# A fused attention and two-layer MoE kernel: the planner's transfer costs, the due times of v and the release of weight loads

## The chip, the cores and the metric

The kernel runs on one core of a Trainium2 chip. The metric is the device time of one execution in microseconds (us). The core's engines run side by side and meet through semaphores: TensorE (PE, with its weight loads as PEld), VectorE (DVE), ScalarE (ACT), GpSimd (POOL) and SyncE (SP), which here only issues transfers. Each engine takes its own instructions strictly in order.

## The reference

Channel attention over 6016 tokens and 256 channels, and two feed-forward layers on its output. All arrays are float32; the weights of the layers arrive as 8-byte numbers that the kernel converts itself.

```python
qn = q / (norm(q, axis=1) + 1e-6)          # 6016 x 256
kn = k / (norm(k, axis=1) + 1e-6)
a = softmax(kn.T @ qn / tau)               # 256 x 256
x = v @ a                                  # 6016 x 256
h = x @ w_in1;  g = relu(h) ** 2           # 256 -> 2048
x = g @ w_out1                             # 2048 -> 256
h = x @ w_in2;  g = maximum(0.01 * h, h)
out = g @ w_out2
```

## The kernel before

The attention matrix is folded into the first layer's w_in, so that the first layer starts from v. From there on the tokens go through in six groups p of two halves, most of 512 tokens a half (`WIDTH`). For each layer L and group p there is a sweep over eight units g, each of 256 of the 2048 inner channels. A unit multiplies x by its part of w_in in seven products (`F1` to `F7`, a Strassen-like form; each product is three matmuls, since every number is split into a high and a low part), applies the nonlinearity on VectorE and ScalarE, and multiplies by its part of w_out into four banks y that a whole sweep adds up. A unit is 45 matmuls. Only the first sweep (layer 1, group 0) has a plain form with four products and a hand-written order.

Beside the units, each sweep of layer 1 has to make the x of the next group (`prepare_x`): two halves of v are loaded, each in four transfers (`load_v`, L236), transposed on VectorE (L245), combined (L1154, L1157) and split into high and low (L1148 on ScalarE, L116 on VectorE) in the single tile xr. It also takes the y of the group before out of its banks into a tile o (`take_out`) and stores it (`put`); v and o share a pool of three buffers. In the second sweep, each wi tile is loaded back (L1185), its sums are made (`join`, L1190) and it is stored again. The second layer's weights are loaded (`load`, L144), converted on VectorE and ScalarE (`exponent` to `low`, tags wst, ce, cm, whl, wis) and stored, which has to be done before the second layer begins.

All this is ordered ahead of time by a planner in the kernel's Python. Every step is a `Task` with an engine, a cost, a due time and what it depends on; a `Buf` is one use of a buffer from a pool, and `link` makes each use wait for the users of the buffer so many places before it, in order of due times, and not start before the use just before it. `simulate` then plays all engines: an engine takes, of the tasks that are ready, the one that is due first. The unit of time is one matmul. A task's followers on other engines are ready at its end and its `lat` later. The plan's start times give the order in which the instructions are emitted, and so the order on each engine; the planned times themselves are not on the chip.

```python
x = min((x for x in open_[e] if x.ready <= t), key=lambda x: x.due)
...
d.ready = max(d.ready, x.end + (0 if d.engine == e and x.lat < 1 else x.lat))
```

Transfers are tasks on SP. Before the change each has the cost 1 and the flight time `LOAD` = 22, but for the load of x in layer 2, which has 2.5 times 22.

Of the kernel before, what the change touches and what calls it, by code (L numbers as in the profile page):

```python
# [31 lines left out]
def attn_moe_moe2(  # L32
# [16 lines left out]
    T = N // P  # L49
# [249 lines left out]
    ACT, DVE = "ACT", "DVE"  # L299
# [31 lines left out]
    with (  # L331
# [46 lines left out]
        for n, (t0, g) in enumerate(tiles):  # L378
            t = qk.pop(n)
# [69 lines left out]
        y, m, z, r = (small[:, i] for i in range(4))  # L449
# [298 lines left out]


    tasks, lines = [], {}  # L750

    class Buf:

# [5 lines left out]
    class Task:  # L759


        def __init__(self, engine, cost, due, fn, *args, deps=(), alloc=None, uses=(), lat=0.3):
            self.engine, self.cost, self.due, self.fn, self.args = engine, cost, due, fn, args
            self.deps = [x for x in deps if x is not None]
            self.order, self.lat, self.start = [], lat, None
            self.item = None
            if alloc is not None:
                alloc.alloc = self
                alloc.users.append(self)
            for b in uses:  # L770
                b.users.append(self)
            tasks.append(self)
# [12 lines left out]
    def simulate(pe):  # L785
        for x in tasks:
            x.then, x.then_order = [], []
        for x in tasks:
            x.left, x.ready = len(x.deps) + len(x.order), 0
            for d in x.deps:  # L790
                d.then.append(x)
            for d in x.order:
                d.then_order.append(x)
        free = {"DVE": 13, "ACT": 6, "SP": 0, "PE": 0}
        open_ = {e: [] for e in free}
        for x in tasks:
            if not x.left:
                open_[x.engine].append(x)
        n = len(tasks)
        while n:  # L800
            best = None
            for e in ("DVE", "ACT", "SP"):
                if open_[e]:
                    t = max(free[e], min(x.ready for x in open_[e]))
                    if best is None or t < best[0]:
                        best = t, e
            t = pe.when(free["PE"])
            if t is not None and (best is None or t < best[0]):
# [12 lines left out]
            for d in x.then + x.then_order:  # L821
                d.left -= 1
                if x in d.order:
                    d.ready = max(d.ready, t)
                if x in d.deps:
                    d.ready = max(d.ready, x.end + (0 if d.engine == e and x.lat < 1 else x.lat))
                if not d.left and d.engine != "PE":
                    open_[d.engine].append(d)
        return free

    KEEP = 4
    LOAD = 22
    GAPS = {"F2": 1, "F3": 1, "F4": 2}

    class PE:
# [72 lines left out]
    def build(base):  # L908
# [10 lines left out]
        def T(*a, **k):  # L919
            return Task(*a, **k)  # L920
# [18 lines left out]
        def convert(u, due, loaded=None, first=None, pace=4, begin=0):  # L939
# [2 lines left out]
            blocks = u.blocks  # L942
            if loaded is None:
                w = Buf("wst", 3, d(-12))
                t = T("SP", 1, d(-12), u.load, alloc=w, lat=LOAD, deps=[begin] if begin else ())
                deps = [t]
            else:
                w, deps = loaded, ()
# [28 lines left out]
                t = T("ACT", 2.7, d(5), u.round, deps=[t], alloc=to, uses=[cm])  # L977
                t = T("DVE", 3, d(6), u.low, deps=[t], uses=[cm, to])
            if u.kind == "o" or L == 2:
                stores[u.kind, L, g] = T("SP", 1, d(7), u.store, deps=[t], uses=[to], lat=LOAD)  # L980
            return t

        whl_done = {0: None, 1: None}
# [15 lines left out]
        for n in range(NG):  # L999
# [3 lines left out]
            if g + 1 < NG:  # L1003
                pw = {}
                b = wi_b[1, 0, g + 1] = Buf("wi", 3, at0(m["fold"]))
                t = T("PE", 6.4, at0(m["fold"]), lambda g=g, pw=pw: pw.update(enumerate(fold(g + 1))),
                      deps=[whl_done[g + 1], *pw_after], alloc=b, uses=[whl_b[g + 1], eT_b])
                fixed.append(t)
                hi = [T("ACT", 2.1, at0(m["fold_high"] + 2.2 * i), lambda i=i, pw=pw: fold_high(i, *pw[i]), deps=[t], uses=[b])
                      for i in range(KC)]  # L1010
                lo = [T("DVE", 2.5, at0(m["fold_low"] + 2.6 * i), lambda i=i, pw=pw: fold_low(i, *pw[i]), deps=[hi[i]], uses=[b])
                      for i in range(KC)]
                pw_after = lo
                stores["i", 1, g + 1] = T("SP", 1, at0(m["fold_low"] + 6), store_folded, g + 1, deps=lo, uses=[b], lat=LOAD)
# [50 lines left out]
        def finish_plain(L, p):  # L1065
# [4 lines left out]
            for half in range(2):  # L1070
# [8 lines left out]
                else:  # L1079
                    a = T("ACT", 2.7 * s, due, take_out, key, 0, deps=done[L, p, half, 0], alloc=o)  # L1080
                b = T("DVE", 3.1 * s, due + 0.1, take_out, key, 1, deps=done[L, p, half, 1] + [a], uses=[o])
                stores["y", L, p, half] = T("SP", 1, due + 3, put, key, deps=[a, b], uses=[o], lat=LOAD)
                if (L, p) == (1, NP - 1) or p < NP - 1:
                    q = (L, p + 1) if p < NP - 1 else (2, 0)
                    for d, t in enumerate((a, b)):
# [7 lines left out]
        def prepare_x(L, p):  # L1093
# [17 lines left out]
            if L == 1:  # L1111
                vs = []
                for half in range(2):
                    v_b[p, half] = Buf("v", 3, t0 + (46, 76)[half])
                    vs.append(T("SP", 1, t0 + (46, 76)[half], load_v, p, half, alloc=v_b[p, half], lat=LOAD))
                for j, (kc, half) in enumerate(((0, 0), (1, 0), (0, 1), (1, 1))):
                    i = SLOT[kc, half]

# [9 lines left out]
            else:  # L1128
# [1 line left out]
                    new()  # L1130
                    nc.sync.dma_start(raw_x(0, 4), x2_d[p][:, :, :w])

                t = T("SP", 1, t0 + 30, load, alloc=xr, lat=2.5 * LOAD, deps=[stores["y", 1, p, 0], stores["y", 1, p, 1]])
                ready.update(dict.fromkeys(range(4), t))

            def split_x(which, i, j, after):
# [40 lines left out]
        def load_wi(n):  # L1177
            L, p, g = units[n]
            b = wi_b[n] = Buf("wi", 3, base[n - 2] + 0.5)
            if n < 2 * NG:  # L1180
# [18 lines left out]
                    nc.sync.dma_start(wi_d[L, g][:, :, 4:], raw(r["w"][:, :, 4:]))  # L1199

                e = base[n] - 12
                t = T("SP", 1, base[n - 2] + 0.5, load, alloc=b, lat=LOAD, deps=[stores.get(("i", 1, g))])
                xb = Buf("whl", 2, e - 25)
                t = T("DVE", 3, e - 25, join, deps=[t], alloc=xb, uses=[b])
                for i in range(4):
                    t = T("DVE", 1.1, e - 20 + i, lambda i=i: r["s"][i](), deps=[t], uses=[xb])
                t = T("ACT", 2.7, e - 10, high, deps=[t], uses=[xb, b])
                wi_ready[n] = T("DVE", 3, e - 5, lows, deps=[t], uses=[xb, b])
                stores["i", 1, g, "s"] = T("SP", 1, e, store, deps=[wi_ready[n]], uses=[b], lat=LOAD)
# [6 lines left out]
            wi_ready[n] = T("SP", 1, base[n - 2] + 0.5, load, alloc=b, lat=LOAD, deps=[dep])  # L1216

        def load_wo(n):
            L, p, g = units[n]
# [2 lines left out]
            if form_of(n) == "P":  # L1222
                def load():
                    src = wo_d[L, g]
                    if L == 2 and g in SG:
                        src = src[:, :, :4].rearrange("p a (k b) m -> p a k b m", k=KC)
                    nc.sync.dma_start(raw(wo_tile(L, p, g)), src)

                wo_ready[L, p, g] = T("SP", 1, base[n] + 13, load, alloc=b, lat=LOAD, deps=[dep])
                return  # L1230

            def load():
# [11 lines left out]
            wo_ready[L, p, g] = T("SP", 1, base[n] + 13, load, alloc=b, lat=LOAD, deps=[dep])  # L1244
            b = wo_b[n, "S1"] = Buf("ws", 2, base[n] + 20)
            wo_ready[n, "S1"] = T("SP", 1, base[n] + 20, load_s1, alloc=b, lat=LOAD, deps=[dep])
            b = wo_b[n, "S23"] = Buf("ce", 2, base[n] + 60)
            wo_ready[n, "S23"] = T("SP", 1, base[n] + 60, load_s23, alloc=b, lat=LOAD, deps=[dep])


        def unit(n):
# [109 lines left out]
            b = g_b[n, "B22"] = Buf("wst", 3, t0 + 50)  # L1361
            t = T("ACT", A1, t0 + 50, cast1, "B22", 1, 1, deps=[n12], alloc=b, uses=[cb[1]])
            low_of[n, "B22"] = b22 = T("DVE", D1, t0 + 57, low1, "B22", 1, 1, deps=[t], uses=[b, cb[1]])
            t1 = T("DVE", D1, t0 + 59, sub, (0, 0), (1, 0), (0, 0), deps=[n22, g0], uses=cb)
            t3 = T("DVE", D1, t0 + 61, sub, (1, 0), (1, 1), (1, 0), deps=[n12, t1], uses=cb[1:])
            t2 = T("DVE", D1, t0 + 65, sub, (1, 1), (1, 1), (0, 0), deps=[t3, b22], uses=cb)
            t4 = T("DVE", D1, t0 + 67, sub, (0, 1), (0, 1), (1, 1), deps=[t2], uses=cb)
# [117 lines left out]
        def combine(p):  # L1485
# [27 lines left out]
            for half, parts in enumerate(((("X", 0, y21), ("P1", 1, y11)), (("V", 0, y22), ("U", 1, y12)))):  # L1513
# [3 lines left out]
                for i, (which, d, dep) in enumerate(parts):  # L1517
# [7 lines left out]
                T("SP", 1, t0 + 80 + 20 * half, put, key, deps=ts_, uses=[o], lat=LOAD)  # L1525

        conv = [Unit(kind, 2, g) for g in range(NG) for kind in "io"]
        for sweep in range(2 * NP):
# [65 lines left out]
```

## Time and profile before

| | |
|---|---|
| median of 3 runs | 1059.78 us (1057.22 to 1061.51) |
| the profiled execution's own time | 1059.12 us |
| its span, first to last instruction | 1057.3 us |
| TensorE busy | 98% |
| TensorE's weight loads | 83% |
| ScalarE busy | 69% |
| VectorE busy | 64% |
| mean granted TensorE clock | 0.994 |

The times are those of whole executions; the profile is of one more, taken by the hardware profiler, and its times count from the first instruction. The shares are means over the span, which holds stages with different loads, so they are read by stage.

### The profile page before, as it was taken

The page shows a single profiled execution, that of the slowest core. Times are in us where ns is not written, and L with a number is a line of the kernel's source. Part 1 is how long each engine was busy: PE and PEld are TensorE (multiplying, and loading weights), DVE is VectorE, ACT ScalarE, POOL GpSimd, SP SyncE. Part 2 cuts the span into 40 slices and gives each one's busy share as a digit, 9 for nine tenths or more (in the row PEclk, how much of TensorE's full clock was granted, in tenths as well). Part 3 has the DMA queues.
Part 4 walks back from the last instruction along what each step waited for, and adds up shares of the span by engine and source line. Part 5 has one row for each costly group of instructions (what it writes and reads, how often), then busy time and mean ns, then how long its engine had stood idle before and what let it go on. Part 6 is the DMA issues. An engine that isn't in the chain of part 4 may idle for free.

```text
span 1057.3 us, 12620 instructions
## 1 busy us (share of the span) xinstructions
PE 1036.2 (98%) x4768; PEld 875.5 (83%) x4768; DVE 673.2 (64%) x917; ACT 728.6 (69%) x1080; POOL 0.7 (0%) x6
## 2 busy tenths in 40 slices
PE   9999999998999999899999999999999999999997
PEld 8888887886887888798888888888888888998886
DVE  5999879997998844656346456546536546544433
ACT  6797877787878775668667567566667657665653
POOL 0000000000000000000000000000000000000000
PEclk9999999999999999899999999999999999999999
DMA  9685497598789547446346445545536544645521
GB/s 359 248 219 182 158 300 245 167 346 244 273 314 276 217 158 208 140 161 238 131 144 209 144 165 188 166 140 188 184 121 205 161 141 163 184 153 165 177 75 40
DMA packets 108156, 203.46 MB, mean 192 GB/s; under 512 B 48576, under 2 KB 52160, under 8 KB 106432
## 3 DMA queue, kind: packets, MB, share of 16 engines
q1 hardware_dynamic: 107376, 202.01, 58.4%
q8 instruction: 37, 0.61, 0.3%
q10 hardware_dynamic: 720, 0.66, 0.2%
q14 instruction: 23, 0.19, 0.1%
HBM read 165.15 MB, written 37.49 MB: 192 GB/s over the span
## 4 chain that ended last, share of the span: by engine, by line
PE 91%; DMA 4%; DVE 2%; SPq 1%; ACT 1%; issue 0%; DVEq 0%
PE y L557 43%; PE ha L557 11%; PE hc L557 10%; PE hb L557 8%; PE he L557 8%; PE h L713 4%; PE sT L399 4%; DMA v<-in_v_dram 4%; PE y L597 2%; SPq L236 1%; PE pw L265 1%; DVE xr L245 1%; DMA wi<-wi 1%; PE warm L364 0%; DVE c L564 0%
## 5 line engine op out<-in xcount | busy, mean ns | idle before, releaser
L557 PE MATMUL y<-g,wo 128*128 128x512 f32 (+1 forms) x2208 | 556.4, 386 | 0.0
L557 PEld LDWEIGHTS y<-g,wo 128*128 128x128 f32 x2208 | 415.2, 188 | 77.7
L116 DVE TENSOR_TENSOR g<-c,g 128x1024 fp32r<-128x1024 f32 (+1 forms) x192 | 229.9, 1200 | 59.0 <-ACT g L683 57.8
L683 ACT CAST g<-c 128x1024 fp32r<-128x1024 f32 (+1 forms) x192 | 198.4, 1034 | 5.2
L557 PE MATMUL ha<-x,wi 128*128 128x512 f32 (+1 forms) x528 | 147.3, 387 | 9.4 <-ACT w L1270 9.4
L557 PE MATMUL hc<-x,wi 128*128 128x512 f32 (+1 forms) x528 | 146.9, 386 | 0.0
L700 ACT ACTIVATE c<-c 128x512 f32<-128x512 f32 (+1 forms) x144 | 89.6, 622 | 58.3 <-DVE c L566 58.2
L557 PEld LDWEIGHTS ha<-x,wi 128*128 128x128 f32 x528 | 98.8, 189 | 28.8 <-ACT w L1270 10.2
L698 ACT ACTIVATE c<-c 128x512 f32<-128x512 f32 (+1 forms) x160 | 98.1, 620 | 29.6 <-DVE c L564 28.1
L557 PEld LDWEIGHTS hc<-x,wi 128*128 128x128 f32 x528 | 99.1, 189 | 18.8 <-ACT c L1270 0.6
L557 PE MATMUL he<-x,wi 128*128 128x512 f32 (+1 forms) x396 | 110.0, 386 | 3.3 <-DVE c L564 3.3
L557 PE MATMUL hb<-x,wi 128*128 128x512 f32 (+1 forms) x396 | 110.4, 387 | 1.2 <-DVE c L564 1.2
L557 PEld LDWEIGHTS he<-x,wi 128*128 128x128 f32 x396 | 74.0, 188 | 18.6 <-DVE c L564 4.6
L557 PEld LDWEIGHTS hb<-x,wi 128*128 128x128 f32 x396 | 74.5, 189 | 15.8 <-DVE c L564 1.8
L1270 ACT COPY w<-hc 128x512 f32<-128x512 f32 (+1 forms) x44 | 25.4, 577 | 48.4 <-PE hc L557 48.4
L1270 ACT COPY w<-ha 128x512 f32<-128x512 f32 (+1 forms) x44 | 25.4, 577 | 48.1 <-PE ha L557 48.1
L566 DVE TENSOR_TENSOR c<-w,hb 128x512 f32<-128x512 f32 (+1 forms) x24 | 16.2, 677 | 63.7 <-ACT w L1270 63.7
L566 DVE TENSOR_TENSOR c<-w,he 128x512 f32<-128x512 f32 (+1 forms) x24 | 16.2, 676 | 62.0 <-ACT w L1270 62.0
L1148 ACT CAST x<-xr 128x1024 fp32r<-128x1024 f32 (+3 forms) x44 | 40.5, 926 | 17.0 <-DVE xr L245 16.8
L713 PE MATMUL h<-x,wi 128*128 128x512 f32 x192 | 47.9, 391 | 0.0
L116 DVE TENSOR_TENSOR x<-xr,x 128x1024 fp32r<-128x1024 f32 (+3 forms) x44 | 46.7, 1064 | 1.6 <-ACT x L1148 1.5
L399 PE MATMUL sT<-qk 128*128 128x256 f32 x188 | 42.4, 388 | 0.0
(112 smaller groups left out, 850.0 us busy)
## 6 DMA issues: line engine op xcount, KB each, us to landing
wi<-wi SPq DMA_DIRECT2D x80, 896.0 KB, 5.9
wo<-wo SPq DMA_DIRECT2D x96, 512.0 KB, 3.4
wi<-wi SPq DMA_DIRECT2D x24, 512.0 KB, 4.6
wst<-in_moe_w_in_dram SPq DMA_DIRECT2D x16, 512.0 KB, 5.9
wst<-in_moe_w_out_dram SPq DMA_DIRECT2D x16, 512.0 KB, 5.0
wi<-wis SPq DMA_DIRECT2D x8, 1024.0 KB, 6.3
x<-o SPq DMA_DIRECT2D x20, 256.0 KB, 5.9
xr<-x SPq DMA_DIRECT2D x5, 1024.0 KB, 4.8
```

The costliest lines, as they stand in the source:

```text
L116: tt(lo, x, raw(hi), op=ALU.subtract)
L236: nc.sync.dma_start(v_t[p, half][b * B : (b + 1) * B, :n], src)
L399: nc.tensor.matmul(sT[j][:, :C], t[:, 0, i, j * P : (j + 1) * P], t[:, 1, i], start=n == 0 and i == 0, stop=last_tile and i == g - 1,)
L557: nc.tensor.matmul(ps, a[m], b[n], start=first and i == 0, stop=i == 2, skip_group_check=True)
L566: tt(to, a, b, op=ALU.add)
L597: nc.tensor.matmul(y_bank(L, p, 1, t // 2)[:, t % 2 * C : (t % 2 + 1) * C], gt[:, a, fb, t * P : (t + 1) * P], wo[:, b, :, fb], start=(g, ...
L683: nc.scalar.copy(g_t[n, half][:, 0, :, :w], c)
L698: nc.scalar.activation(c, c, AF.Square)
L700: nc.scalar.activation(c, c, AF.Prelu, alpha=0.01)
L713: nc.tensor.matmul(h_t[n, half, fb][:, :w], a[i], b[j], start=start, stop=stop, skip_group_check=True)
L1148: nc.scalar.copy(part(0), src())
L1270: nc.scalar.copy(to, h(0))
```

## The change

SP's tasks get a cost and a flight time by kind: `COST` is what the issue takes of SP, `LAT` the time to landing, both in units of the plan. The old numbers at the calls are replaced by the name of the kind. The due times of the two halves of v go from 46 and 76 to 30 and 60 units after the start of the sweep that loads them. A task can have a `release`, before which the planner does not start it, and the loads of the second layer's weights get one. POOL joins the engines that the planner plays, and four subtractions get their cost written out.

```diff
     tasks, lines = [], {}
+    COST = {"v": 10, "out": 9, "y": 5, "wi": 2.6, "wo": 1.6, "wst": 2, "store": 2, "x": 1.6}
+    LAT = {"v": 50, "wi": 34, "wo": 26, "wst": 36, "store": 34, "x": 55}
...
-        def __init__(self, engine, cost, due, fn, *args, deps=(), alloc=None, uses=(), lat=0.3):
+        def __init__(self, engine, cost, due, fn, *args, deps=(), alloc=None, uses=(), lat=0.3, release=0):
+            if engine == "SP":
+                cost, lat = COST.get(cost, 2.3), LAT.get(cost, 30)
...
-            x.left, x.ready = len(x.deps) + len(x.order), 0
+            x.left, x.ready = len(x.deps) + len(x.order), x.release
...
-        free = {"DVE": 13, "ACT": 6, "SP": 0, "PE": 0}
+        free = {"DVE": 13, "ACT": 6, "POOL": 0, "SP": 0, "PE": 0}
...
-            for e in ("DVE", "ACT", "SP"):
+            for e in ("DVE", "ACT", "POOL", "SP"):
...
+    VDUE = 30, 60
...
-                t = T("SP", 1, d(-12), u.load, alloc=w, lat=LOAD, deps=[begin] if begin else ())
+                t = T("SP", "wst", d(-12), u.load, alloc=w, lat=LOAD, deps=[begin] if begin else (),
+                      release=d(-12) - 60 if begin else 0)
...
-                stores["y", L, p, half] = T("SP", 1, due + 3, put, key, deps=[a, b], uses=[o], lat=LOAD)
+                stores["y", L, p, half] = T("SP", "out" if L == 2 else "y", due + 3, put, key, deps=[a, b], uses=[o], lat=LOAD)
...
-                    v_b[p, half] = Buf("v", 3, t0 + (46, 76)[half])
-                    vs.append(T("SP", 1, t0 + (46, 76)[half], load_v, p, half, alloc=v_b[p, half], lat=LOAD))
+                    v_b[p, half] = Buf("v", 3, t0 + VDUE[half])
+                    vs.append(T("SP", "v", t0 + VDUE[half], load_v, p, half, alloc=v_b[p, half], lat=LOAD))
...
-                t = T("SP", 1, base[n - 2] + 0.5, load, alloc=b, lat=LOAD, deps=[stores.get(("i", 1, g))])
+                t = T("SP", "wi", base[n - 2] + 0.5, load, alloc=b, lat=LOAD, deps=[stores.get(("i", 1, g))])
...
-                wo_ready[L, p, g] = T("SP", 1, base[n] + 13, load, alloc=b, lat=LOAD, deps=[dep])
+                wo_ready[L, p, g] = T("SP", "wo", base[n] + 13, load, alloc=b, lat=LOAD, deps=[dep])
...
-            t1 = T("DVE", D1, t0 + 59, sub, (0, 0), (1, 0), (0, 0), deps=[n22, g0], uses=cb)
+            t1 = T("DVE", 3 * s, t0 + 59, sub, (0, 0), (1, 0), (0, 0), deps=[n22, g0], uses=cb)
```

The other transfers are changed in the same way as those shown: the stores get the kind "store", the loads of x in layer 2 the kind "x", the remaining loads of wi and wo theirs. The conversions of the second layer's weights keep their own due times.

## Rows read from the trace of the kernel before

**Rows 1.** The page's busy times: us, share of the span, instructions.

```profile
PE 1036.2 (98%) x4768; PEld 875.5 (83%) x4768; DVE 673.2 (64%) x917; ACT 728.6 (69%) x1080; POOL 0.7 (0%) x6
```

**Rows 2.** Busy time by stage: length, PE, PEld, DVE, ACT, POOL (instructions), clock, DMA share, GB/s.

```profile
224.00:306.00 82.00, 78.00 (x343) 63.81 (x342) 72.25 (x113) 64.91 (x99) 0.00 (x0) 1.00 0.86 286
...
462.00:1050.00 588.00, 588.00 (x2725) 498.41 (x2724) 306.33 (x357) 377.50 (x560) 0.00 (x0) 1.00 0.48 158
```

**Rows 3.** TensorE in order of time: start, duration; idle before in brackets.

```profile
160.93 0.96 PE L557 MATMUL he<-x,wi 128*128 128x512 f32 x3 [0.97 <-DVE c L564]
...
243.69 0.96 PE L557 MATMUL he<-x,wi 128*128 128x512 f32 x3 [1.52 <-DVE c L564]
...
256.66 0.98 PE L557 MATMUL ha<-x,wi 128*128 128x512 f32 x3 [2.48 <-ACT w L1270]
...
329.94 0.96 PE L557 MATMUL he<-x,wi 128*128 128x512 f32 x3 [0.81 <-DVE c L564]
...
340.25 0.97 PE L557 MATMUL hb<-x,wi 128*128 128x512 f32 x3 [1.18 <-DVE c L564]
...
427.81 1.49 PE L557 MATMUL ha<-x,wi 128*128 128x448 f32 x3 [6.95 <-ACT w L1270]
```

**Rows 4.** Busy time by stage around the longest gap, columns as in rows 2.

```profile
427.80:433.40 5.60, 5.59 (x15) 4.99 (x16) 4.49 (x7) 3.89 (x6) 0.00 (x0) 0.51 0.11 13
433.40:450.00 16.60, 16.60 (x83) 15.07 (x82) 9.01 (x11) 11.77 (x20) 0.00 (x0) 1.00 0.60 219
```

**Rows 5.** Waits of VectorE: who for whom, us in total, times, longest.

```profile
DVE xr L245 <- DMA v<-in_v_dram: 18.8, 6, 8.0
...
DVE wr L1190 <- DMA wi<-wi: 2.6, 2, 2.1
```

**Rows 6.** SP in order of time: issues of two halves of v.

```profile
328.74 1.90 SPq L236 DMA_DIRECT2D v<-in_v_dram  x4
...
413.48 5.35 SPq L236 DMA_DIRECT2D v<-in_v_dram  x4
```

**Rows 7.** VectorE in order of time: the first transposes of these halves.

```profile
336.16 0.65 DVE L245 STREAM_TRANSPOSE xr<-v 128x448 f32<-128x448 f32 x1 [1.70 <-DMA v<-in_v_dram]
...
424.94 1.31 DVE L245 STREAM_TRANSPOSE xr<-v 128x512 f32<-128x512 f32 x2 [7.96 <-DMA v<-in_v_dram]
```

**Rows 8.** TensorE in order of time: twelve matmuls and the next start.

```profile
231.80 2.88 PE L557 MATMUL y<-g,wo 128*128 128x512 f32 x12
234.52 0.84 PE L557 MATMUL hc<-x,wi 128*128 128x512 f32 x3
```

**Rows 9.** The view of DMA issues: count, KB each, median us to landing.

```profile
wst<-in_moe_w_in_dram SPq DMA_DIRECT2D x16, 512.0 KB, 5.9
...
v<-in_v_dram SPq DMA_DIRECT2D x32, 128.0 KB, 6.3
```

**Rows 10.** SP in order of time at the start of the first layer.

```profile
53.71 4.92 SPq L236 DMA_DIRECT2D v<-in_v_dram  x8
58.73 0.71 SPq L144 DMA_DIRECT2D wst<-in_moe_w_in_dram  x1
```

**Rows 11.** VectorE's groups, shapes apart: count, busy us, mean ns, idle before.

```profile
L159 DVE SCALAR_TENSOR_TENSOR cm<-wst,cm 128x512 f32<-128x512 uint32 x32 | 22.0, 689 | 0.5
...
L116 DVE TENSOR_TENSOR wis<-wr,wis 128x1024 fp32r<-128x1024 f32 x8 | 9.8, 1220 | 0.4 <-ACT wis L205 0.4
```

**Rows 12.** Busy time by stage, columns as in rows 2.

```profile
50.00:145.00 95.00, 94.98 (x462) 79.94 (x463) 85.36 (x148) 79.19 (x119) 0.00 (x0) 1.00 0.64 193
...
208.00:345.00 137.00, 131.01 (x574) 107.08 (x573) 120.34 (x187) 109.32 (x167) 0.00 (x0) 1.00 0.87 285
345.00:450.00 105.00, 98.05 (x440) 84.11 (x439) 59.99 (x79) 68.70 (x108) 0.00 (x0) 0.95 0.57 179
```

**Rows 13.** VectorE in order of time around the start of the second group.

```profile
141.45 1.22 DVE L116 TENSOR_TENSOR x<-xr,x 128x1024 fp32r<-128x1024 f32 x1
...
160.79 0.69 DVE L747 COPY o<-y 128x512 f32<-128x512 f32 x1
```

More of the change, by code (lines that the diff above doesn't have):

```diff
@@ L759, in attn_moe_moe2 @@
     class Task:
-        def __init__(self, engine, cost, due, fn, *args, deps=(), alloc=None, uses=(), lat=0.3):
+        def __init__(self, engine, cost, due, fn, *args, deps=(), alloc=None, uses=(), lat=0.3, release=0):
+            if engine == "SP":
+                cost, lat = COST.get(cost, 2.3), LAT.get(cost, 30)
             self.engine, self.cost, self.due, self.fn, self.args = engine, cost, due, fn, args
             self.deps = [x for x in deps if x is not None]
-            self.order, self.lat, self.start = [], lat, None
+            self.order, self.lat, self.start, self.release = [], lat, None, release
             self.item = None
@@ L979, in convert @@
             if u.kind == "o" or L == 2:
-                stores[u.kind, L, g] = T("SP", 1, d(7), u.store, deps=[t], uses=[to], lat=LOAD)
+                stores[u.kind, L, g] = T("SP", "store", d(7), u.store, deps=[t], uses=[to], lat=LOAD)
             return t
@@ L1013, in build @@
                 pw_after = lo
-                stores["i", 1, g + 1] = T("SP", 1, at0(m["fold_low"] + 6), store_folded, g + 1, deps=lo, uses=[b], lat=LOAD)
+                stores["i", 1, g + 1] = T("SP", "store", at0(m["fold_low"] + 6), store_folded, g + 1, deps=lo, uses=[b], lat=LOAD)
                 wi_ready[1, 0, g + 1] = lo[-1]
@@ L1131, in load @@
                     nc.sync.dma_start(raw_x(0, 4), x2_d[p][:, :, :w])
-                t = T("SP", 1, t0 + 30, load, alloc=xr, lat=2.5 * LOAD, deps=[stores["y", 1, p, 0], stores["y", 1, p, 1]])
+                t = T("SP", "x", t0 + 30, load, alloc=xr, lat=2.5 * LOAD, deps=[stores["y", 1, p, 0], stores["y", 1, p, 1]])
                 ready.update(dict.fromkeys(range(4), t))
@@ L1208, in load_wi @@
                 wi_ready[n] = T("DVE", 3, e - 5, lows, deps=[t], uses=[xb, b])
-                stores["i", 1, g, "s"] = T("SP", 1, e, store, deps=[wi_ready[n]], uses=[b], lat=LOAD)
+                stores["i", 1, g, "s"] = T("SP", "store", e, store, deps=[wi_ready[n]], uses=[b], lat=LOAD)
                 return
@@ L1215, in load_wi @@
             dep = stores["i", 1, g, "s"] if L == 1 else stores["i", 2, g]
-            wi_ready[n] = T("SP", 1, base[n - 2] + 0.5, load, alloc=b, lat=LOAD, deps=[dep])
+            wi_ready[n] = T("SP", "wi", base[n - 2] + 0.5, load, alloc=b, lat=LOAD, deps=[dep])
         def load_wo(n):
@@ L1242, in load_s23 @@
                 nc.sync.dma_start(raw(t), wo_d[L, g][:, :, 6:])
-            wo_ready[L, p, g] = T("SP", 1, base[n] + 13, load, alloc=b, lat=LOAD, deps=[dep])
+            wo_ready[L, p, g] = T("SP", "wo", base[n] + 13, load, alloc=b, lat=LOAD, deps=[dep])
             b = wo_b[n, "S1"] = Buf("ws", 2, base[n] + 20)
-            wo_ready[n, "S1"] = T("SP", 1, base[n] + 20, load_s1, alloc=b, lat=LOAD, deps=[dep])
+            wo_ready[n, "S1"] = T("SP", "wo", base[n] + 20, load_s1, alloc=b, lat=LOAD, deps=[dep])
             b = wo_b[n, "S23"] = Buf("ce", 2, base[n] + 60)
-            wo_ready[n, "S23"] = T("SP", 1, base[n] + 60, load_s23, alloc=b, lat=LOAD, deps=[dep])
+            wo_ready[n, "S23"] = T("SP", "wo", base[n] + 60, load_s23, alloc=b, lat=LOAD, deps=[dep])
         def unit(n):
@@ L1363, in unit @@
             low_of[n, "B22"] = b22 = T("DVE", D1, t0 + 57, low1, "B22", 1, 1, deps=[t], uses=[b, cb[1]])
-            t1 = T("DVE", D1, t0 + 59, sub, (0, 0), (1, 0), (0, 0), deps=[n22, g0], uses=cb)
-            t3 = T("DVE", D1, t0 + 61, sub, (1, 0), (1, 1), (1, 0), deps=[n12, t1], uses=cb[1:])
-            t2 = T("DVE", D1, t0 + 65, sub, (1, 1), (1, 1), (0, 0), deps=[t3, b22], uses=cb)
-            t4 = T("DVE", D1, t0 + 67, sub, (0, 1), (0, 1), (1, 1), deps=[t2], uses=cb)
+            t1 = T("DVE", 3 * s, t0 + 59, sub, (0, 0), (1, 0), (0, 0), deps=[n22, g0], uses=cb)
+            t3 = T("DVE", 3 * s, t0 + 61, sub, (1, 0), (1, 1), (1, 0), deps=[n12, t1], uses=cb[1:])
+            t2 = T("DVE", 3 * s, t0 + 65, sub, (1, 1), (1, 1), (0, 0), deps=[t3, b22], uses=cb)
+            t4 = T("DVE", 3 * s, t0 + 67, sub, (0, 1), (0, 1), (1, 1), deps=[t2], uses=cb)
             b = g_b[n, "G1"] = Buf("g", 4, t0 + 74)
@@ L1524, in combine @@
                     ts_.append(T("DVE", 3.1 * s, t0 + 120 + 30 * half + 15 * i, go, deps=[dep, *ts_], **k))
-                T("SP", 1, t0 + 80 + 20 * half, put, key, deps=ts_, uses=[o], lat=LOAD)
+                T("SP", "out", t0 + 80 + 20 * half, put, key, deps=ts_, uses=[o], lat=LOAD)
         conv = [Unit(kind, 2, g) for g in range(NG) for kind in "io"]
```

## The prediction

> **What bounds the kernel now.** I read the page's busy shares first [rows 1]: TensorE is busy 1036.2 of 1057.3 us. The planner's whole work is to keep it fed, so a change of order can win only what TensorE still loses. I then asked for busy time by stage [rows 2]: from 462 us to 1050 us TensorE has no idle time at all, and between 50 and 145 us 0.02 us [rows 12]. What is lost lies between 145 and 450 us. The timeline of TensorE there [rows 3] shows six gaps, in brackets: 0.97, 1.52, 2.48, 0.81, 1.18 and 6.95 us, together 13.91 us. The long one has a second price: the granted clock is 0.51 of full from 427.8 to 433.4 us, which is the lower of the two levels (1.2 against 2.4 GHz), after TensorE stood idle from 420.9 us [rows 4]. Its 15 matmuls took 5.6 us, where the next stretch at full clock does 83 in 16.6 us, so 15 in 3.0 us: 2.6 us more. So 16.5 us are to be had between the two ends of the span, and no more.
>
> Why the gaps are there. The waits of VectorE [rows 5] show it: 18.8 us in 6 waits for the v transfer in front of the transposes of L245, and 2.6 us for a reload of wi in front of L1190. VectorE runs in its planned order, so behind a transpose that waits stand the adds (L564) and behind these ScalarE's copy w, for which TensorE's next product waits. The releaser named in a gap is that copy or add, but its own cause is the v transfer. The gaps at 243.69, 256.66, 329.94, 340.25 and 427.81 us each lie behind such a wait; the one at 160.93 us lies behind the wi reload.
>
> Why v is late: the SP timeline shows when the four issues of a half of v begin, VectorE's timeline when the first transpose that waits can start. The shortest and longest of six are 328.74 to 336.16 us (7.4 us) and 413.48 to 424.94 us (11.5 us) [rows 6, 7]. The planner's unit is one matmul: it charges 3 for three, and twelve take 234.52 − 231.80 = 2.72 us [rows 8], so 0.227 us. The old plan gives v 1 for the issue and 22 for the flight, 5.2 us: 2 to 6 us too little each time.
>
> **The change part by part.**
>
> *v.* Four issues are now charged 10 units and the flight 50: 60 units, 13.6 us, over the longest of the six (11.5 us) by 2.1 us. VectorE's transposes are therefore planned behind the landing and other work stands ahead of them. The due times 46 and 76 become 30 and 60, and that alters more than rank. The pool v has three buffers, given out in order of due time; the line of a sweep is now v0, o0, v1, o1 in place of o0, v0, o1, v1 (o are the two taken-out halves of y, due at 44 and 74). A due time does not hold an issue back, so v0 may go as soon as o1 of the sweep before has begun and its third-last buffer is free, most of a sweep early; v1 goes once o0 has begun, at about 44 units (10 us) into the sweep where it waited for 74 and for o0's store. Both land before VectorE can want them. On SP the loads of wi and wo stand behind these issues; what v0 waits for there, the store of an o taken out a sweep before, has landed by its planned place, and if it had not, they would be held by that remainder against some 20 us of slack that a wi load has (it is asked for two units ahead). Five gaps go: 1.52 + 2.48 + 0.81 + 1.18 + 6.95 = 12.94 us, and the clock's 2.6 us with the last. If the cover failed in the sweep with the longest gap alone, 9.6 us would come back.
>
> A rule can be weighed here. The row of the page gives a v transfer 6.3 us from issue to landing for 128 KB, four in a row [rows 9]. The Trainium skill ("DMA: Bandwidth & Descriptors", section on the anatomy of one DMA) gives about 2.0 us and the bytes over 436 GB/s, from the GpSimd path; by it the 512 KB of a half would need an estimated 3.2 us. By that price the old allowance of 5.2 us was enough and this part would bring 0; by the rows it brings 15.5 us.
>
> *wi, wo, wst, store, x.* wi goes from 1 + 22 units (5.2 us) to 2.6 + 34 (8.3 us); the longest wait for its reload was 2.1 us [rows 5], which the 3.1 us more cover. This takes the 0.97 us gap, because SP's real time for v and wst ahead of it is now in the plan. A later planned arrival costs nothing while it is under that slack. Bounds: 0 to 0.97 us gained; I take 0.97, since nothing else stands in that gap. For wo, wst and stores nothing in the rows waits long, so 0 either way; x keeps its flight of 55.
>
> *SP at the start.* With v of the next group due earlier than any o, three halves are free to go at once where the trace shows two: eight issues take 4.92 us from 53.71 us, and the weight load behind starts at 58.73 us [rows 10]. Four more add 2.5 us to that load, the folded store and what follows. Bounds 0 to 2.5 us; I take 0: the planner puts a weight load 48 units (10.9 us) ahead of the first step on it, its flight is 5.9 us [rows 9], and the 5.0 us between them cover the delay. TensorE loses 0.02 us in that stage [rows 12]; without the cover it would be the 2.5 us.
>
> *Second layer's weights.* Sixteen conversions kept their due times but ran as soon as VectorE was free; each load now also has an earliest time, 60 units before its due time (a rule of the plan; the chip waits for nothing new). By the code they run from about 208 us (72 units before the second sweep, whose stretch is the first of [rows 2]) to about 550 us. A conversion of w_in is nine steps of at most 0.69 us and one of 1.22 us [rows 11], at most 7.4 us; one of w_out is six steps, at most 4.1 us: 92 us for the eight pairs at most. VectorE was busy 120.34 of 137 us (88%) in 208 to 345 us and 59.99 of 105 (57%) in 345 to 450 us [rows 12]; 92 us over 342 us is 27% more, so at most 84% throughout. TensorE kept its pace at 88% wherever v did not hold VectorE, so I price this at 0; the bound on the bad side is one new gap like the shorter ones, 0.8 to 2.5 us, in the stretch to 550 us.
>
> *POOL, subtract costs.* No task is ever given to POOL, the subtractions belong to a form that no unit has (SG is empty), and their new cost equals the old: 0.
>
> **The sum.** 12.94 + 0.97 + 2.6 = 16.5 us off the profiled execution's 1059.1 us gives 1042.6 us. New plans tend to leave a small wait somewhere; I add one of the size of the smaller gaps, 1 us: 1043.6 us. The median of the runs is 0.7 us above the profiled execution, so 1044 us.
>
> **The rivals.**
>
> A, part of it stays (1048 to 1054 us). One sweep still waits, by a v landing that takes over 13.6 us, or since conversions and transposes meet in it. The longest wait, 8.0 us, is long beside the other five, 10.8 us together [rows 5], so landings have a tail. Price: the last gap with its clock, 6.95 + 2.6 = 9.6 us, gives 1053 us; the two middle gaps of the second sweep, 4.0 us, 1048.
>
> B, no change (1054.5 to 1065 us). v would land no later than planned anyway and the gaps come from elsewhere: VectorE, freed of the wait, meets a wait of the same length for the wst or wi transfers, so the adds stay late: 1059 us. For it speaks that the transfers share the queue; against it that VectorE waited 2.6 us in all for wi against 18.8 for v [rows 5]. It is also what the skill's transfer price named above would give; the 7.4 to 11.5 us of [rows 6, 7] stand against that.
>
> C, slower (over 1065 us). The new line of buffers makes o1 take the buffer of v0, so o1 waits for v0's transposes. These need the one xr tile, which is free when x of the sweep before is split. If VectorE comes to them only at their due time (118 units into the sweep against 74 for o1), the y banks of the second half are taken out 10 us late in each of the four sweeps that load v. TensorE can run other products over some 10 us of that; each us beyond it is paid four times, and above 4.1 us a sweep (16.5 / 4) the gain is gone; at 6 us with a fall of the clock in each (2.6 us) it would be 1059 − 16.5 + 34 = 1077 us. Against it: in the first sweep, the tightest, x was split by 142.7 us and the o copy came at 160.79 us [rows 13], 18 us in which to fit two transposes of 0.7 us [rows 7].
>
> **How the numbers follow.** A difference of 0.5% (5.3 us) is about what a measurement of this kernel can tell from no change. Chances: forecast (1040 to 1048 us) 0.70, A 0.13, B 0.09, C 0.08. So faster 0.83, same 0.09, slower 0.08. TensorE's work alone puts the floor at 1042.6 us, or 1040 with the 2 us by which runs scatter; the upper end takes in A's dearest case, 1053 us. That holds 0.70 and nearly all of A, so 8 in 10.
>
> **What would show it.** Right: VectorE's wait for v falls from 18.8 us to under 3 us; TensorE's idle between 145 and 450 us falls from 13.9 to under 3 us and the granted clock is 1.00 in all of it; v0 is issued long before its sweep's transposes, v1 about 10 us into its sweep; VectorE's share is between 70 and 85% from 208 to 550 us. The forecast is wrong if a gap of over 3 us stands in any sweep; C is right if ahead of the gaps an o copy waits for an L245 transpose, B if L149 or L1190 waits where L245 did.

## The result and the profile after

The changed kernel takes 1041.74 us (median of 4 runs, 1040.62 to 1042.18), the kernel before 1058.68 us beside it. The ratio is 0.9835 (95% interval 0.9811 to 0.9859): 16.9 us or 1.65% faster. The forecast was 1044 us. The profiled execution took 1040.62 us, with a span of 1038.8 us, 18.5 us shorter than that of before. Of all the executions below one, of "all but what belongs to v", took 5765 us at a granted clock of 0.168; it was the profiled one, so that kernel has a median of three runs and no trace.

The page's busy times, and the slices of TensorE and of its granted clock:

```profile
PE 1031.5 (99%) x4768; PEld 873.0 (84%) x4768; DVE 675.0 (65%) x917; ACT 729.0 (70%) x1080; POOL 0.7 (0%) x6
...
PE   9999999999999999999999999999999999999997
...
PEclk9999999999999999999999999999999999999999
```

Beside [rows 1] TensorE's share goes from 98% to 99%. All 40 slices show 9 in both lines but TensorE's last, where the kernel runs out.

Busy time by stage in the changed kernel, columns as in [rows 2]:

```profile
142.00:224.00 82.00, 82.00 (x363) 67.79 (x362) 64.36 (x106) 63.94 (x98) 0.00 (x0) 1.00 0.66 198
224.00:306.00 82.00, 82.00 (x363) 67.30 (x362) 62.32 (x87) 64.30 (x96) 0.00 (x0) 1.00 0.74 236
306.00:388.00 82.00, 82.00 (x363) 67.79 (x362) 60.54 (x87) 62.44 (x96) 0.00 (x0) 1.00 0.76 246
388.00:462.00 74.00, 74.00 (x361) 67.54 (x361) 59.26 (x87) 58.63 (x96) 0.00 (x0) 1.00 0.78 264
462.00:1033.00 571.00, 571.00 (x2649) 483.00 (x2647) 308.03 (x367) 368.12 (x544) 0.00 (x0) 1.00 0.50 164
```

In the stretch of [rows 2] from 224 to 306 us TensorE was busy 78.00 of 82.00 us; now it is busy in all of it and in every other stretch shown, at the full clock. All TensorE's waits of the changed kernel (who for whom, us in total, times, longest) lie in the attention part, before 51 us:

```profile
PE warm L364 <- DVE small L358: 1.1, 1, 1.1
PE eT L492 <- ACT e L486: 0.3, 1, 0.3
```

The six gaps of [rows 3] are gone. So is their cause: the row of VectorE's waits in which L245 waits for v, 18.8 us in [rows 5], does not exist any more, nor that of the wi reload. In the changed kernel transfers held VectorE up only in these two lines:

```profile
DVE o L747 <- DMA x<-o: 1.3, 1, 1.3
DVE ce L149 <- DMA wst<-in_moe_w_in_dram: 1.2, 2, 0.8
```

### The profile page after: what moved, and what is told of

It is laid out like the page before. It is cut to its first block, busy times and chain, and to the rows that moved or that the text cites. A ratio compares the mean times of both kernels' runs of the same rounds, so it can differ in the third digit from the quotient of the medians.

```text
span 1038.8 us, 12601 instructions
## 1 busy us (share of the span) xinstructions
PE 1031.5 (99%) x4768; PEld 873.0 (84%) x4768; DVE 675.0 (65%) x917; ACT 729.0 (70%) x1080; POOL 0.7 (0%) x6
## 4 chain that ended last, share of the span: by engine, by line
PE 97%; DMA 2%; ACT 0%; DVE 0%; ACTq 0%; SPq 0%; issue 0%
PE y L557 47%; PE ha L557 11%; PE hc L557 11%; PE hb L557 8%; PE he L557 8%; PE h L713 4%; PE sT L399 2%; PE y L597 2%; PE pw L265 1%; DMA qk<-in_k_dram 1%; DMA qk<-in_q_dram 1%; ACT e L486 0%; ACTq L351 0%; PE pn L373 0%; SPq L351 0%
## 5 line engine op out<-in xcount | busy, mean ns | idle before, releaser
L557 PEld LDWEIGHTS hc<-x,wi 128*128 128x128 f32 x528 | 98.5, 188 | 18.8 <-ACT c L1276 0.8
L557 PEld LDWEIGHTS ha<-x,wi 128*128 128x128 f32 x528 | 98.4, 188 | 18.8 <-ACT c L1276 1.0
L399 PE MATMUL sT<-qk 128*128 128x256 f32 x188 | 42.6, 388 | 0.1
L713 PEld LDWEIGHTS h<-x,wi 128*128 128x128 f32 x192 | 35.6, 188 | 7.3 <-DVE wi L285 0.2
```

Source lines behind the costliest of these rows:

```text
L399: nc.tensor.matmul(sT[j][:, :C], t[:, 0, i, j * P : (j + 1) * P], t[:, 1, i], start=n == 0 and i == 0, stop=last_tile and i == g - 1,)
L557: nc.tensor.matmul(ps, a[m], b[n], start=first and i == 0, stop=i == 2, skip_group_check=True)
L713: nc.tensor.matmul(h_t[n, half, fb][:, :w], a[i], b[j], start=start, stop=stop, skip_group_check=True)
```

## The experiments

Three theories stood against each other. The one that the prediction rests on: VectorE stands, in its fixed order, at transposes whose v the plan believes landed, so what counts is v's planned landing against its real one. "Due times": the early issue, through the new line of buffers, is what counts. "Pace": VectorE was too full while it converted the second layer's weights, and an emptier one would make up for a late v. Each ratio is to the kernel before, measured in the same set; its medians in the four sets were 1058.68, 1058.86, 1059.33 and 1059.96 us. The last two columns are from the kernel's trace; a gap is idle time of TensorE after 51 us.

| kernel | median, us | ratio (95% interval) | VectorE's wait for v, us | TensorE's gaps, us |
|---|---|---|---|---|
| before | 1058.68 | 1 | 18.8 | 13.9 |
| the change | 1041.74 | 0.9835 (0.9811 to 0.9859) | 0 | 0 |
| v's cost and flight alone | 1040.46 | 0.9816 (0.9800 to 0.9832) | 0 | 0 |
| v's due times alone | 1048.04 | 0.9891 (0.9866 to 0.9917) | 5.5 | 4.5 |
| v's cost, flight and due times | 1041.92 | 0.9832 (0.9813 to 0.9851) | 0 | 1.3 |
| v's issue cost alone | 1050.45 | 0.9912 (0.9886 to 0.9937) | 8.6 | 5.4 |
| v's flight alone | 1043.65 | 0.9848 (0.9822 to 0.9874) | 1.6 | 1.3 |
| v's flight 1 unit | 1085.88 | 1.0240 (1.0223 to 1.0256) | 42.6 | 29.1 |
| earliest times alone | 1061.99 | 1.0021 (1.0008 to 1.0034) | 12.5 | 14.3 |
| earliest times, weights' costs | 1050.05 | 0.9910 (0.9885 to 0.9935) | 13.7 | 7.1 |
| all but what belongs to v | 1050.42 | 0.9918 (0.9894 to 0.9943) | no trace | no trace |
| all but the earliest times | 1041.63 | 0.9827 (0.9810 to 0.9843) | 1.7 | 0.8 |
| wi's cost and flight alone | 1056.08 | 0.9954 (0.9936 to 0.9972) | 15.7 | 10.5 |
| the change, transposes planned late | 1048.25 | 0.9889 (0.9861 to 0.9916) | 0 | 3.7 |

The gaps are TensorE's idle time in the views by stage, from 51 to 600 us; they agree with the idle brackets of its timeline, as in [rows 3], to 0.3 us. A gap behind a reload of wi is counted too.

### v's cost and flight alone

```diff
-COST: v 1     LAT: v 22
+COST: v 10    LAT: v 50          (all other costs, due times and loads as before)
```

> Only v's cost and flight in the plan are new (10 and 50 units); due times, pace and all other costs are those of before. Theory (VectorE stands at transposes whose v is planned to land 2 to 6 us too early): the five gaps behind v go, 12.9 us, and the clock's 2.6 us with the longest; the 0.97 us behind the wi reload may stay: 1041 to 1045 us, VectorE's wait for v under 1 us. Rival 'due times' (the early issue from the new line of buffers is what counts): most gaps stay, 1050 us or more. Rival 'pace' (VectorE was too full while the weights were converted): 1055 us or more.

Measured: 1040.46 us, as fast as the whole change. The waits of VectorE for transfers are these, none for v:

```profile
DVE wr L1196 <- DMA wi<-wi: 1.1, 2, 0.8
...
DVE ce L149 <- DMA wst<-in_moe_w_in_dram: 0.5, 1, 0.5
```

and its busy time by stage, columns as in [rows 2], shows that it is as full as ever, 127.04 of 137 us, while the weights are converted, and TensorE loses nothing beside it:

```profile
208.00:345.00 137.00, 137.00 (x606) 113.30 (x605) 127.04 (x199) 113.70 (x173) 0.00 (x0) 1.00 0.87 294
345.00:450.00 105.00, 105.00 (x493) 92.08 (x492) 61.87 (x76) 75.29 (x120) 0.00 (x0) 1.00 0.60 197
```

So two numbers of the plan carry the gain, and a full VectorE is no cause. The gap behind the wi reload went with them, though wi's own numbers are the old ones here: VectorE still waits there, 1.1 us in two waits, but TensorE no longer feels it.

One step of the theory does not hold as it was put. The plan lets 13.6 us pass from the issue to the transposes, but on the chip the later half of v in a sweep had less. SP's wait, its issue, and VectorE's transposes of the earlier half (first) and the later half in this kernel:

```profile
SPq L236 <- DVE xr L245: 13.4, 2, 7.6
```

```profile
247.78 1.93 SPq L236 DMA_DIRECT2D v<-in_v_dram  x4
```

```profile
246.45 1.30 DVE L245 STREAM_TRANSPOSE xr<-v 128x512 f32<-128x512 f32 x2
...
254.44 0.70 DVE L245 STREAM_TRANSPOSE xr<-v 128x512 f32<-128x512 f32 x1
```

The issue of the later half waits on SP for the transposes of the earlier half, a wait that the prediction did not read from the code. The kernel before has it too, 1.4 us in two waits; here it is 13.4 us in two. The later half was then transposed 6.7 us after its issue, and the next such half 6.1 us after, and VectorE did not wait for either: they landed sooner than any of the six halves of before (7.4 to 11.5 us). So in two sweeps the larger numbers move the transposes back, and with them the next issue, and what is issued then lands faster. In the 6.6 us behind it the DMA moved 186 GB/s, where in the 8.8 us behind the same issue in the kernel before it moved 303; whether that is why it lands faster isn't shown.

### How much is enough: v's issue cost, v's flight, and none

```diff
-COST: v 1     LAT: v 22          (23 units, 5.2 us from issue to planned landing)
+COST: v 10    LAT: v 22          (first kernel: 32 units, 7.3 us)
+COST: v 1     LAT: v 50          (second: 51 units, 11.6 us)
+COST: v 1     LAT: v 1           (third: 2 units, 0.5 us)
```

> Only v's issue cost is new (10 units in place of 1), its flight stays 22, all else is that of before: 32 units or 7.3 us from issue to planned landing, where the six measured ones that VectorE waited for took 7.3 to 11.3 us. Theory (what counts is planned landing against real landing): the waits shrink to what lies over 7.3 us, some 0 to 4 us each, so a part of the gaps stays: 1042 to 1050 us; and the gap at the wi reload goes, since SP's time for v ahead of it is now planned. Rival 'flight alone' (the issue cost changes nothing): 1055 us or more.

> Only v's flight is new (50 units in place of 22), its issue cost stays 1: 51 units or 11.6 us, over the longest of the six (11.3 us). Theory: VectorE's waits for v go, but SP's 2 to 3 us for v stay unplanned, so the gap of about 1 us behind the wi reload stays: 1041 to 1045 us, with VectorE waiting some 2 us at L1196 (join). Rival 'issue alone': 1050 us or more.

> Only v's flight is new, and in the wrong direction: 1 unit in place of 22, so the plan puts the transposes up to 4.8 us earlier still; due times and all else are those of before. Theory: VectorE waits up to 4.8 us longer at each of eight halves of v, 25 to 55 us in all, TensorE loses most of what is added and its clock falls more often: 1068 to 1095 us. Rivals 'due times' and 'pace': as before, 1055 to 1063 us.

VectorE's waits at L245 in the three, in this order:

```profile
DVE xr L245 <- DMA v<-in_v_dram: 8.6, 3, 3.9
```

```profile
DVE wr L1196 <- DMA wi<-wi: 2.2, 1, 2.2
...
DVE xr L245 <- DMA v<-in_v_dram: 1.6, 1, 1.6
```

```profile
DVE xr L245 <- DMA v<-in_v_dram: 42.6, 8, 8.3
```

With planned landings 0.5, 5.2, 7.3, 11.6 and 13.6 us after the issue, VectorE waits 42.6, 18.8, 8.6, 1.6 and 0 us, and the times are 1085.9, 1058.7, 1050.5, 1043.7 and 1040.5 us: one row of doses. The gaps behind v are 29.1, 12.9, 5.4, 0.2 and 0 us, so TensorE loses 0.6 to 0.7 us for each us that VectorE stands, and hardly anything at the smallest dose. The first of the three came out just over its expected 1050 us. Neither the issue cost alone nor the flight alone is what counts: each takes a part. In the second, where SP's time for v is not in the plan, the wait for the wi reload in front of L1196 (the join, L1190 in the kernel before) is 2.2 us and TensorE's gap behind it 1.1 us, as expected; in the first, with that time in the plan, no gap stands there.

The doses are the plan's. On the chip the one wait that is left in the second kernel came at an issue that had stood behind the transposes of the earlier half; SP's line, then VectorE's:

```profile
331.12 1.91 SPq L236 DMA_DIRECT2D v<-in_v_dram  x4
```

```profile
335.78 0.65 DVE L245 STREAM_TRANSPOSE xr<-v 128x448 f32<-128x448 f32 x1 [1.63 <-DMA v<-in_v_dram]
```

This half had landed 4.7 us after its issue, where the plan had given it 11.6.

### v's due times alone

```diff
-VDUE = 46, 76
+VDUE = 30, 60          (all costs and flights as before)
```

> Only v's due times are new (30 and 60), with the old costs and flights. Theory: the first half of v is issued a sweep early and lands in time, so the 1.52 and 0.81 us go; the second half is issued earlier but its transposes are planned earlier by as much, so the gaps behind it (2.48, 1.18 and 6.95 us with its clock) stay in some size: 1050 to 1058 us. Rival 'due times': all gaps behind v go, 1041 to 1045 us. Rival 'pace': 1055 us or more.

Measured: 1048.04 us, better than expected. VectorE's waits for v and wi:

```profile
DVE xr L245 <- DMA v<-in_v_dram: 5.5, 3, 2.7
DVE wr L1196 <- DMA wi<-wi: 3.9, 2, 2.2
```

The first halves are issued a sweep early and none is waited for; the three waits are at second halves (2.3, 2.7 and 0.6 us). They are shorter than I expected, since the second halves now start where the first ones did. So the early issue is a second way to the same end, worth 10.8 us of the 18.4 by the medians. What it leaves is not all v's: of the 4.5 us of gaps 2.0 us (before the matmuls at 160.69 and 170.70 us) lie behind the two reloads of wi, ahead of the first wait for v.

### Everything of v

```diff
-COST: v 1     LAT: v 22     VDUE = 46, 76
+COST: v 10    LAT: v 50     VDUE = 30, 60
```

> Everything of v (cost 10, flight 50, due times 30 and 60), all else as before. Theory: with the costs right the due times add nothing more, 1039 to 1043 us, no gap of TensorE over 0.5 us after 50 us.

Measured: 1041.92 us, as expected but for one gap. The due times add nothing to the costs. The gap is not v's: VectorE, which no longer waits for v, waits for the reload of wi. That wait and TensorE's gap behind it:

```profile
DVE wr L1196 <- DMA wi<-wi: 2.9, 2, 2.4
```

```profile
170.71 0.97 PE L557 MATMUL hb<-x,wi 128*128 128x512 f32 x3 [1.28 <-DVE c L564]
```

### The even pace, without and with the weights' own costs

```diff
-t = T("SP", ..., u.load, ...)                                  # weights: 1 and 22
+t = T("SP", ..., u.load, ..., release=d(-12) - 60)             # first: 1 and 22
+t = T("SP", ..., u.load, ..., release=d(-12) - 60)             # second: 2 and 36
```

> Only the earliest times of the second layer's weight loads are new, so that VectorE is less full from 208 to 345 us; v and all costs are those of before. Theory: VectorE still waits at v's transposes as long as before, 1055 to 1062 us. Rival 'pace': VectorE makes up for the waits, 1041 to 1048 us.

> The earliest times of the second layer's weight loads together with the new cost and flight of these loads (2 and 36); v and the rest as before. With the earliest times alone VectorE waited 17.1 us for these loads. Theory: those waits go and what is left is the waits for v, so about the time of before or a little under, 1050 to 1060 us. Rival 'pace' (an even pace lets VectorE make up for late v): 1046 us or less.

The waits of VectorE for transfers with the pace alone:

```profile
DVE ce L149 <- DMA wst<-in_moe_w_in_dram: 13.2, 5, 4.7
DVE xr L245 <- DMA v<-in_v_dram: 12.5, 4, 4.5
...
DVE ce L149 <- DMA wst<-in_moe_w_out_dram: 3.9, 2, 3.3
```

and with the weights' costs as well:

```profile
DVE xr L245 <- DMA v<-in_v_dram: 13.7, 6, 5.3
...
DVE ce L149 <- DMA wst<-in_moe_w_in_dram: 1.4, 2, 0.7
```

Alone, the pace gains nothing (ratio 1.0021, inside the expected range). In the kernel before, VectorE stood 0.5 us in all for these weights; now each comes just in time by a plan that lets it fly 5.0 us, and VectorE stands 17.1 us at L149. Its waits for v did not stay as long as expected: they fell from 18.8 to 12.5 us. With 2 and 36 units the waits for the weights shrink to 1.4 us, and v's remain. The rest of the row is only half explained: against the kernel before, VectorE waits 13.7 in place of 18.8 us for v and TensorE loses 7.1 in place of 13.9 us, more of a gain than the shorter waits would give at 0.6 to 0.7, even with the 1 us of the gap behind the wi reload, which is gone too. So an emptier VectorE may help by some us, or the new order meets shorter waits by luck (the longest is 5.3 us where it was 8.0); these runs don't part the two.

### All but v, and all but the pace

```diff
 first kernel: the whole change, but COST: v 1, LAT: v 22, VDUE = 46, 76
 second kernel: the whole change, but
-                      release=d(-12) - 60 if begin else 0)
+                      release=0)
```

> The whole change without what belongs to v: v keeps cost 1, flight 22 and the due times 46 and 76; all other costs and flights and the earliest times of the weight loads are new. Theory: as the earliest times with the weights' own costs, that is some 14 us of waits for v on VectorE and 1046 to 1054 us. Rival 'the other kinds count' (wi, wo, stores, outputs): 1044 us or less.

> The whole change without the earliest times: the second layer's weights are converted as early as VectorE can. Theory: no gap comes back, 1040 to 1044 us, VectorE busy some 90% from 208 to 345 us. Rival 'pace': gaps of several us come back in that stretch, 1048 us or more.

Without v's numbers the rest of the change is worth 0.8% (ratio 0.9918), about what the pace with the weights' costs gave (0.9910); so wi, wo, the stores and the outputs do not carry the change. Without the pace the time is that of the whole change, with VectorE busy 93% from 208 to 345 us. One wait for v is left there. SP's timeline (start, duration of four issues) and then VectorE's show two halves, the one before it and the one it is for:

```profile
232.82 7.17 SPq L236 DMA_DIRECT2D v<-in_v_dram  x4
...
250.40 4.79 SPq L236 DMA_DIRECT2D v<-in_v_dram  x4
```

```profile
247.76 1.29 DVE L245 STREAM_TRANSPOSE xr<-v 128x512 f32<-128x512 f32 x2
...
261.46 1.17 DVE L245 STREAM_TRANSPOSE xr<-v 128x448 f32<-128x448 f32 x2 [1.75 <-DMA v<-in_v_dram]
```

The first half's issues alone took 7.17 us. The fourth began at 236.33 us and landed 10.5 us later, 14.0 us after the first began, over the plan's 13.6; the transposes, 14.9 us after the first issue, were just not held. The second half was transposed 11.1 us after its first issue and held VectorE 1.75 us: less than the 13.6 us of the plan, so its issue came late against the plan. SP issued without a pause of over 0.1 us from 232.82 us to that issue, so the slow first half ahead of it on SP is the likely cause; no run takes it away alone.

### wi's cost and flight alone

```diff
-COST: wi 1      LAT: wi 22
+COST: wi 2.6    LAT: wi 34
```

> Only the cost and flight of the wi transfers are new (2.6 and 34 in place of 1 and 22). Prediction's step: the gap of 0.97 us behind the reload of wi in the first sweep after group 0 goes, all gaps behind v stay, 1056 to 1060 us. Rival: that gap comes from SP's unplanned time for v ahead of the reload and stays.

Measured: 1056.08 us, 0.5% under before. VectorE has no wait for the reload, but those for v are there; and TensorE is busy all of the stretch that held the gap (columns as in [rows 2]):

```profile
DVE xr L245 <- DMA v<-in_v_dram: 15.7, 5, 5.5
```

```profile
145.00:208.00 63.00, 63.00 (x279) 52.08 (x278) 56.94 (x98) 50.52 (x79) 0.00 (x0) 1.00 0.74 238
```

So that small gap has two cures: wi's own allowance, or v's cost on SP. The prediction named both.

### Rival C on purpose

```diff
-ready[i] = T("DVE", 3.1 * s, due(), go, deps=..., **k)
+at = due()
+ready[i] = T("DVE", 3.1 * s, at, go, deps=..., release=at, **k)
```

> The whole change, and VectorE's transposes of v are not planned before their due times (118 units into the sweep and later), while the taking out of the second half of y (due 74) needs the buffer that the first two of them empty. This is rival C of the prediction put on purpose. If its mechanism holds, the taking out comes some 15 us late in four sweeps and TensorE runs dry in them: 1055 us or more. If the planner can feed TensorE other products meanwhile, 1040 to 1046 us.

Measured: 1048.25 us, between the two. The copy of the second half of y on ScalarE (L747), first in the changed kernel, then here, and here the transposes on VectorE that free its buffer:

```profile
155.61 0.59 ACT L747 COPY o<-y 128x512 f32<-128x512 f32 x1 [0.28 <-PE y L557]
```

```profile
175.64 0.58 ACT L747 COPY o<-y 128x512 f32<-128x512 f32 x1
```

```profile
169.51 0.70 DVE L245 STREAM_TRANSPOSE xr<-v 128x512 f32<-128x512 f32 x1
...
174.87 0.70 DVE L245 STREAM_TRANSPOSE xr<-v 128x512 f32<-128x512 f32 x1
```

The buffer's line works as the prediction read it from the code: the copy stands behind the second transpose and comes 20 us late, and 22 to 23 us late in the other three sweeps. But TensorE does not run dry for what lies beyond the 10 us that the prediction allowed: its gaps are 3.7 us in all, 2.5 of them in the first of the four sweeps, and the time is 6.5 us over that of the change by the medians. So TensorE had other products to run for nearly all of the delay.

## Why the prediction was right, and where its terms were off

**The cause.** Right, and shown from both sides: more allowance for v removes waits and gaps in step, less adds to them. What the prediction had as one fixed time, 7.4 to 11.5 us from issue to landing, is not fixed: halves took from 4.7 us to 14.0 us, and in the kernel with v's costs alone two of them were covered because they landed within 6.7 us, not because they were given the planned 13.6 us. That VectorE's order and not the amount of its work was the trouble is shown by v's costs alone, with VectorE at 93% from 208 to 345 us.

**Which edit.** Half right. I gave the 15.5 us to v's costs and due times together. The costs alone give all of it; the due times alone give 10.8 us by the early issue, and nothing on top of the costs in time. The early issue is seen in the changed kernel: SP's timeline first, then VectorE's first transposes.

```profile
54.09 7.92 SPq L236 DMA_DIRECT2D v<-in_v_dram  x12
62.11 0.71 SPq L144 DMA_DIRECT2D wst<-in_moe_w_in_dram  x1
...
147.81 3.00 SPq L236 DMA_DIRECT2D v<-in_v_dram  x4
...
161.68 2.13 SPq L236 DMA_DIRECT2D v<-in_v_dram  x4
...
231.70 2.51 SPq L236 DMA_DIRECT2D v<-in_v_dram  x4
...
248.38 1.90 SPq L236 DMA_DIRECT2D v<-in_v_dram  x4
```

```profile
142.75 1.30 DVE L245 STREAM_TRANSPOSE xr<-v 128x512 f32<-128x512 f32 x2
...
167.88 0.70 DVE L245 STREAM_TRANSPOSE xr<-v 128x512 f32<-128x512 f32 x1
...
197.60 0.70 DVE L245 STREAM_TRANSPOSE xr<-v 128x512 f32<-128x512 f32 x1
...
247.06 1.29 DVE L245 STREAM_TRANSPOSE xr<-v 128x512 f32<-128x512 f32 x2
```

Three halves start at 54.09 us; the third is transposed at 142.75 us. The half issued at 161.68 us is transposed at 197.60 us, that of 231.70 us at 247.06 us, 15.4 us later, where 13.6 us were planned and the old plan gave 5.2. Over the halves behind the first three the shortest such distance is 15.4 us, where with v's costs alone it is 6.1 us: the due times buy room, which these runs did not need. In the sweeps that begin near 224 and 306 us, v1 is issued some 8 us in, about as foretold. The next v0 goes most of a sweep early, as foretold, but at 248.38 us it had waited 4.9 us on SP for the transposes of v1 (247.06 us), which the prediction did not have, and its own transposes follow 17 us behind: the planner brought them forward with it. Rival C's lead is there too: the transposes at 142.75 us are done before the copy of 155.61 us needs their buffer.

**The size.** The sum said 16.5 us off, less 1 us for a new small wait. The medians give 16.9 us and the two profiled executions 18.5 us. No new wait came, so that term was 0. But the price of a gap was too small, and with it the 16.5 us that were all there was to be had: the idle bracket of [rows 3] counts from the end that is modelled for the matmul before (the page's mean duration is 386 ns, while the next starts after 227 ns, [rows 8]), which leaves out 0.16 us; and the three matmuls behind a gap take 0.96 us ([rows 3]) where others take 0.84 ([rows 8]), 0.12 us more. At six gaps that is 1.6 us: 13.9 + 1.6 + 2.6 = 18.1 of the 18.5 us. Runs of one kernel scatter by 2 to 4 us, so this agreement is in part luck; the price of a single gap is read from the rows.

**SP at the start.** Right for TensorE, though the delay was larger: twelve issues take 7.92 us where eight took 4.92 [rows 10], and the weight load starts at 62.11 in place of 58.73 us, 3.4 us later where 2.5 was the bound. TensorE's busy time in 50 to 145 us is 94.85 us against 94.98 [rows 12], and the difference lies before 51 us, in the attention part.

**The pace.** Priced at 0, and 0 it is within the whole change: with and without it the medians are 1041.74 and 1041.63 us. VectorE's busy time by stage in the changed kernel, columns as in [rows 2]:

```profile
50.00:145.00 95.00, 94.85 (x463) 79.70 (x462) 86.51 (x151) 79.14 (x120) 0.00 (x0) 1.00 0.66 194
...
208.00:345.00 137.00, 137.00 (x604) 112.62 (x603) 103.01 (x147) 105.91 (x160) 0.00 (x0) 1.00 0.77 239
345.00:450.00 105.00, 105.00 (x494) 92.21 (x493) 79.37 (x117) 80.55 (x128) 0.00 (x0) 1.00 0.71 243
450.00:540.00 90.00, 90.00 (x408) 76.23 (x407) 63.01 (x83) 70.11 (x107) 0.00 (x0) 1.00 0.64 221
```

It is 75, 76 and 70% in the three stretches from 208 to 540 us, within the 70 to 85% foretold, where [rows 12] had 88 and 57%. What the prediction missed is that the pace by itself makes new waits: it turns the weights into transfers just in time, and the weights' own new cost and flight time keep VectorE from standing there (17.1 against 1.4 us).

**The transfer's price.** By the price in the Trainium skill ("DMA: Bandwidth & Descriptors", section on the anatomy of one DMA), an estimated 3.2 us for a half of v, the old 5.2 us were enough. The waits of before say otherwise, and the shortest that VectorE waited for in any kernel took 4.7 us. That price is for one transfer on another path and says nothing of four in a row beside other traffic; the measurement decides.

**The rivals.** A did not come in the changed kernel. Without the pace it came in small: one half landed later than its 13.6 us, the half behind it came late against the plan, VectorE waited 1.7 us for that one and TensorE lost 0.5 us. B did not come: in the changed kernel no wait for a wst or wi transfer is over 0.8 us. The nearest to it is everything of v alone, where reloads of wi held VectorE 2.9 us (2.6 in the kernel before) and TensorE lost 1.3 us behind them; in the whole change that wait is gone. C is a true mechanism at the wrong price: with each us beyond 10 paid four times, 20 us late would have cost some 40 us, and it cost 6.5.

## What to carry to other kernels

Where engines run a planned order, look for waits of an engine on a transfer whose allowance in the plan is smaller than issue to landing in the trace; everything behind that instruction is late with it, and the engine named as the releaser of the gap is often only the last link. Measure the allowance from the first issue to the landing of the last of several transfers, on a stretch with traffic, and charge the issuing queue its time as well. Then read the distance from issue to first use again in the new trace: the chip can hold an issue for something that the plan does not know, and the planned margin is used up before the transfer starts. A step that is moved to just in time needs its true flight time in the plan first; where the bound engine is full, a further spreading of the work gains nothing.

## What the runs showed of the hardware

The same four issues of v take SP as little as 1.90 us [rows 6] and as much as 7.17 us (the row at 232.82 us above). That longest one fell in a stretch of 22 us with a DMA share of 0.93, 273 GB/s; but in the same stretch of the changed kernel the share is 0.99 and four issues took 2.51 us, so the mean share alone does not tell when an issue is slow.

The last of the four transfers of a half of v landed from 4.7 us (v's flight alone, issued at 331.12 us) to 14.0 us (all but the earliest times, issued at 232.82 us) after the first issue began. What sets this time isn't shown.

A gap of TensorE costs some 0.28 us more than its idle bracket, as worked out above, even where the granted clock stays at 1.00.
